# Moving two scans, one count and a few products inside a 24-step recurrent kernel

## The chip, the cores and the metric

The kernel runs on one core of a Trainium2 chip. The metric is the device time of one execution in microseconds (us). A core has five engines that run side by side, each through its own queue in order: TensorE (PE; its weight loads are shown as PEld), VectorE (DVE), ScalarE (ACT), GpSimd (POOL) and SyncE (SP). A unit waits for another only through semaphores. Matmul results land in a small memory of their own, PSUM, and are read from there by DVE and ACT; all other tiles lie in SBUF.

## The reference, cut to what matters

Three stages are computed on the host's inputs: a recurrent attention over 768 steps for 4 x 8 heads of width 40, a mixture of 8 experts over its 3072 output rows, and a feed-forward layer with a squared ReLU.

```
for t in range(S):                                  # S = 768, state is [B, H, D, D]
    y[:, :, t] = einsum('bhd,bhde->bhe', r_t, state)
    Sa = einsum('bhde,bhe->bhd', state, a_t)
    state = state * w_t[:, :, None, :] - einsum('bhd,bhe->bhde', Sa, b_t)
    state = state + einsum('bhd,bhe->bhde', v_t, k_t)

logits = x @ w_gate                                 # x = y, laid out as [3072, 320]
expert = argmax(logits); gate = softmax(logits)[expert]
pos[i] = number of earlier rows of the same expert  # rows beyond the capacity are dropped
out[i] = gate[i] * relu(x[i] @ w1[expert]) @ w2[expert]

h = maximum(out @ w_in, 0.0); result = (h * h) @ w_out
```

The change concerns the first stage, and of the second only the counting behind `pos`.

## The kernel before, in words

The 768 steps are cut into 24 chunks of 32 steps (c = 0 to 23), and `Attention.run` writes every engine's instructions out by hand, chunk by chunk; no scheduler moves them. Chunks 1 to 19 are written by the inner function `chunk(c)`, and chunk 0 and chunks 20 to 23 by the code behind it. `m = c % 4` is the place in a group of four.

In one chunk TensorE goes through the same list of products, each into a PSUM tile named in the trace: `pu` (L399), `py` (L489, the output of the chunk before), `pk` (transposes, L341), `G` (L192, the Gram product for the chunk seven ahead), `ps` (L418, the new state), `pv` (L455), `pq` (L467, scores), `px` (L385, the block product with the inverse, in `solve`), `gpt` (L845), `pa` (L341), `pn` (L441) and `pl` (L861, gate logits). DVE and ACT carry the results on: `gram_mask` reads G into `GM` and `N` (L205, L206), `state_decay` reads ps into `ru` (L429), `gate_in` reads py into `xt` (L498), `scores_mask` reads pq (L475); ACT copies pv to `vut` (L458), px to `lu` (L388), pl to `lg` (L862).

Four things set the order around the change.

- **The inverse.** Each group of four chunks needs one inverse of triangular blocks. When the last G of the group is masked, in the chunk with m = 0, `inv_start` transposes GM (L214) and prepares 27 products; `inv` then does a number of them (a product L265 and its sum L269, both on DVE, each needing the one before) at the end of the chunks with m = 0, 1 and 2. `PLAN` gives the numbers: 13, 9, 3 and, after `choose`, 2. With the last one `inv_end` writes `TT` (L304), which ACT copies into `TB` (L313, `block_T`) for px. `FIRST` is the plan of the first group and is not changed.
- **Scans and scalings.** `scan(c + 8)` does two running products over a tile `e` and its partner `wB` on DVE (L157, L160, L162, L163), and `scale` multiplies three parts of `e` on POOL (L178), once per chunk. The four quarters of the next `e` are loaded by four DMAs that ACT's queue issues (`load`, L138).
- **The gate's batches.** Rows are ranked in batches. At m = 3 of chunks 3, 7, 11 and 15 a batch is counted: `choose` (L882 to L890, DVE) at the end of the chunk before, `count` in the chunk (an exponential on ACT L895, eight matmul passes into `pc` L899, a copy on ACT L901), and `rank` and `rank_batch` (small DVE instructions, L908 to L938) at its end.
- **Small PSUM tiles.** py, pc, pq, gpt and pl come from `small`, which hands out two buffers in turn. So each of these tiles has to wait until the tile two before it in the program has been read.

Of the kernel before, what the change touches and what calls it, by code (L numbers as in the profile page):

```python
# [35 lines left out]
class Attention:  # L36
# [91 lines left out]
    def load(self, c, part=None):  # L128
        if c >= NC:
            return  # L130
        if not part:
            self.st["E", c] = self.eb(c % 8, [104, 2048], F32)
        e = self.st["E", c]
        if part is None:
            self.nc.sync.dma_start(e, self.E[c][:, 0:2048])
        else:
            s = slice(512 * part, 512 * part + 512)
            self.nc.scalar.dma_start(e[:, s], self.E[c][:, s])  # L138
# [373 lines left out]

    def run(self, extra, weights):
        LA, SHIFT = 7, 20
        PLAN, FIRST = (13, 9, 3, 2), (9, 10, 6, 2)
        V, G = self.nc.vector, self.nc.gpsimd
        gate = self.gate

        def fill(c, i):
            if 1 <= c <= 2:  # L520
                extra(5 * c + i, 5 * c + i + 1)
            elif 5 <= c < 14 and i == 2:
                extra(10 + c, 11 + c if c < 13 else None)

        def wload(i):
            r = (self.L, self.Tt)[i % 2].rearrange("p a b -> p (a b)")
            weights.load(i, r[:, 0:704], 1)
# [57 lines left out]
        def chunk(c):  # L585

            m, bt = c % 4, gate.batch(c)
            plan = FIRST if c < 4 else PLAN
            early, nxt = bt if c < 17 else None, gate.batch(c + 1) if c < 16 else None
            self.u(c)  # L590
            if bt and 17 <= c:
                gate.choose(*bt)
            self.y(c - 1)
            self.nat_k(c + 1)
            if m != 3:
                self.block_T(c + 1)
            self.load_r(c + 1)
            self.load(c + LA + 2, 0)
            fill(c, 0)
            self.gram(c + LA)  # L600
            self.gram_mask(c + LA)
            self.state(c)
            self.vu_t(c)
            if m == 3:
                self.block_T(c + 1)
            self.load(c + LA + 2, 1)
            fill(c, 1)
            if early:
                gate.count(*early)
            self.scan(c + LA + 1)  # L610
            self.scale(c + LA + 1)
            self.state_decay(c)
            self.gate_in(c - 1)
            self.scores(c)
            self.scores_mask(c)
            if m == 0:
                self.inv_start(c // 4 + 1, lambda k, h: G)
            self.solve(c + 1)
            self.load_v(c + 2)
            self.store_x(c - 1)  # L620
            self.load_w(c + LA + 4)
            self.load(c + LA + 2, 2)
            fill(c, 2)
            gate.xT(c - 1)
            if bt and 17 <= c:
                gate.count(*bt)
            self.nat_n(c + 2)
            self.nat_a(c + 2)
            self.nat_pc(c + 2)
            self.state_t(c + 1)  # L630
            self.load(c + LA + 2, 3)
            fill(c, 3)
            gate.logits(c - 1)
            if m != 3:
                self.inv("v" * plan[m])
            if nxt:
                gate.choose(*nxt)
            if m == 2:
                self.inv("v" * plan[3])
            if bt:  # L640
                gate.rank(*bt)
                gate.rank_batch(*bt)
            fill(c, 4)
            gate.scatter(1)
            if c == 19:
                wload(0)
                wload(1)
# [5 lines left out]
        for c in range(NC - 1):  # L653
            if 1 <= c < SHIFT:
                chunk(c)
                continue
            m = c % 4
# [90 lines left out]
        c = NC - 1  # L748
# [922 lines left out]
```

## Time and profile before

| | |
|---|---|
| Time, median of 3 runs | 1120.45 us (1119.92 to 1125.08) |
| Profiled execution, its own time | 1126.1 us |
| Its span, first to last instruction | 1124.2 us |
| Busy share of the span: PE, PEld, DVE, ACT, POOL | 83%, 75%, 69%, 50%, 24% |
| From 493.80 us to the end (experts and last layer) | 630.40 us, PE busy 595.29 us |
| Mean granted TensorE clock | 0.904 of full |

In the timelines below a row is one instruction or a run of like ones: start in us from the span's beginning, duration in us, engine, source line, operation, output <- inputs, shape, count, and in brackets the idle time of that engine before it with what ended it. "issue" as what ended it means that the profile shows no instruction whose end released the engine. The idle time in a row of a busy engine matters; that of an engine that nothing waits for does not.

### The profile page before, as it was taken

What the parts mean: (1) busy time and instruction counts of PE and PEld (TensorE: products, weight loads), DVE (VectorE), ACT (ScalarE), POOL (GpSimd) and SP (SyncE); (2) the same over time, 40 slices, a digit from 0 to 9 for tenths busy, and PEclk for the clock granted to TensorE, in tenths of its full rate; (3) what the DMA queues carried; (4) which work ended last, traced back from release to release, by engine and by line L of the source; (5) the groups of instructions that cost most, each with busy time, mean ns of one, the idle gap of its engine ahead of it and who ended that gap; (6) DMA issues with size and microseconds to landing.
All of it is one profiled execution on the core that took longest, in us unless ns stands there. A gap on an engine that the chain in (4) does not pass through costs nothing.

```text
span 1124.2 us, 30643 instructions
## 1 busy us (share of the span) xinstructions
PE 934.6 (83%) x12526; PEld 842.7 (75%) x12526; DVE 774.2 (69%) x1611; ACT 560.4 (50%) x1286; POOL 273.8 (24%) x320
## 2 busy tenths in 40 slices
PE   5247677778666788889889999799999999999995
PEld 3237566667665677768879999798899999999895
DVE  7999979889798795465887888876644344444432
ACT  7135464555463767634545566546634343434432
POOL 5422131222313101013554555423401010000000
PEclk6578888797797988899989999999999999999998
DMA  7736544444442223236765666534100001000000
GB/s 184 194 97 184 172 125 124 124 140 149 115 149 84 87 61 104 79 93 181 222 209 187 208 212 216 178 98 143 50 24 24 24 12 37 1 24 2 19 5 27
DMA packets 80647, 122.71 MB, mean 109 GB/s; under 512 B 9679, under 2 KB 57409, under 8 KB 79561
## 3 DMA queue, kind: packets, MB, share of 16 engines
q1 hardware_dynamic: 71173, 100.09, 30.2%
q10 hardware_dynamic: 7020, 12.78, 3.8%
q0 software_dynamic: 2304, 7.78, 2.2%
q8 instruction: 101, 1.65, 0.6%
q14 instruction: 49, 0.40, 0.1%
HBM read 91.36 MB, written 29.35 MB: 107 GB/s over the span
## 4 chain that ended last, share of the span: by engine, by line
PE 54%; DVE 18%; DMA 6%; issue 6%; ACT 5%; POOL 1%; SPq 1%; ACTq 0%; DVEq 0%; POOLq 0%
PE phg L1334 15%; PE phe L1334 5%; PE pog L1359 5%; PE pog L1360 5%; PE pog L1358 5%; DVE pr L265 4%; PE px L385 3%; DMA xs<-zs_s 2%; PE pq L467 2%; PE poe L1360 2%; PE poe L1358 2%; PE poe L1359 2%; DVE Tt L269 1%; DVE ru L429 1%; DVE Xm L269 1%
## 5 line engine op out<-in xcount | busy, mean ns | idle before, releaser
L1344 DVE SCALAR_TENSOR_TENSOR sqg<-phg,rg 128x512 f32<-128x512 f32 x96 | 66.2, 690 | 119.0 <-ACT rg L1343 119.0
L1343 ACT ACTIVATE rg<-phg 128x512 f32<-128x512 f32 x96 | 57.2, 596 | 110.5 <-PE phg L1334 110.3
L1346 DVE TENSOR_TENSOR hlg<-sqg,hhg 128x512 fp32r<-128x512 f32 x96 | 66.5, 693 | 65.9 <-ACT hhg L1345 63.2
L1345 ACT CAST hhg<-sqg 128x512 fp32r<-128x512 f32 x96 | 59.6, 621 | 78.5 <-DVE sqg L1344 78.5
L1334 PE MATMUL phg<-xhg,e 128*128 128x512 f32 x264 | 93.1, 393 | 0.0
L385 PE MATMUL px<-TB,X 128*104 128x128 f32 x384 | 67.2, 347 | 26.2 <-ACT TB L313 25.0
L388 ACT COPY lu<-px 104x512 f32<-104x512 f32 x48 | 25.7, 588 | 120.5 <-PE px L385 120.5
L385 PEld LDWEIGHTS px<-TB,X 128*104 128x104 f32 x384 | 61.7, 230 | 28.8 <-ACT TB L313 25.4
L467 PE MATMUL pq<-rq,vut 128*64 128x64 f32 x768 | 42.1, 264 | 49.0 <-issue 31.7
L178 POOL TENSOR_TENSOR e<-e 104x512 f32<-104x512 f32 x21 | 27.9, 1331 | 207.4 <-DVE e L163 90.2
L467 PEld LDWEIGHTS pq<-rq,vut 128*64 128x64 f32 x768 | 35.7, 173 | 55.0 <-issue 32.2
L1359 PE MATMUL pog<-e,hhg 128*128 128x320 f32 x240 | 74.1, 309 | 0.0
L1360 PE MATMUL pog<-e,hlg 128*128 128x320 f32 x240 | 74.1, 309 | 0.0
L1358 PE MATMUL pog<-e,hhg 128*128 128x320 f32 x240 | 73.9, 308 | 0.0
L192 PE MATMUL G<-e 64*32 64x64 f32 (+1 forms) x1536 | 27.6, 254 | 49.3 <-issue 29.2
L192 PEld LDWEIGHTS G<-e 64*32 64x32 f32 (+1 forms) x1536 | 20.1, 120 | 59.3 <-issue 33.6
L1152 POOL TENSOR_TENSOR e<-rw,e 128x256 fp32r<-128x256 f32 x51 | 43.0, 846 | 72.3 <-ACT e L1151 71.5
L1334 PE MATMUL phe<-xhe,e 128*128 128x480 f32 (+4 forms) x176 | 59.3, 378 | 0.0
L178 POOL TENSOR_TENSOR e<-e,wB 104x512 f32<-104x512 f32 x42 | 53.4, 1287 | 24.3 <-DVE wB L157 17.1
L1334 PEld LDWEIGHTS phg<-xhg,e 128*128 128x128 f32 x264 | 49.5, 188 | 8.8
L313 ACT COPY TB<-TT 32x256 f32<-32x256 f32 x94 | 37.8, 402 | 35.6 <-DVE TT L304 34.3
L1338 ACT ACTIVATE hhe<-phe 128x480 fp32r<-128x480 f32 (+4 forms) x64 | 33.9, 529 | 38.7 <-PE phe L1334 38.2
(315 smaller groups left out, 2919.5 us busy)
## 6 DMA issues: line engine op xcount, KB each, us to landing
e<-in_E_dram ACTq DMA_DIRECT2D x60, 208.0 KB
rw<-in_w_dram SPq DMA_DIRECT2D x30, 320.0 KB
zs_s<-zt SPq DMA_DIRECT2D x24, 320.0 KB
rw<-in_w_dram SPq DMA_DIRECT2D x30, 256.0 KB
e<-in_E_dram SPq DMA_DIRECT2D x9, 832.0 KB
ru<-in_VR_dram SPq DMA_DIRECT2D x48, 128.0 KB
cr<-in_wi_dram SPq DMA_DIRECT2D x20, 256.0 KB
cr<-in_wo_dram SPq DMA_DIRECT2D x20, 256.0 KB
```

Of the source, the lines that this page charges most:

```text
L178: eng.tensor_tensor(z, z, f, ALU.mult)
L192: T.matmul(gps[32 * g : 32 * g + 32, par, 64 * o : 64 * o + 64], e[r, 32 * i : 32 * i + 32], e[r, 512 + 64 * i : 576 + 64 * i], start=True ...
L385: self.nc.tensor.matmul(px[0:104, par, 128 * o : 128 * o + 128], X[:, par, o, :], TB[:, 4 * par + o, :], start=True, stop=True)
L467: T.matmul(pq[s, 64 * q : 64 * q + 64], vut[:, q, s], rt[:, :, q, pp], start=True, stop=True)
L1334: T.matmul(o, lt, rt, start=(i == 0), stop=(i == len(seq) - 1))
L1343: A.activation(r[:, :n], o, AF.Relu)
L1344: V.scalar_tensor_tensor(sq[:, :n], o, 0.0, r[:, :n], ALU.max, ALU.mult)
L1345: A.copy(hh[:, :n], sq[:, :n])
L1346: V.tensor_tensor(hl[:, :n], sq[:, :n], b32(hh)[:, :n], ALU.subtract)
L1358: T.matmul(o, hh[:, t], W["h2"], start=(f == 0), stop=False)
L1359: T.matmul(o, hh[:, t], W["l2"], start=False, stop=False)
L1360: T.matmul(o, hl[:, t], W["h2"], start=False, stop=(f == NF - 1))
```

## The change

Four edits, all in `Attention`.

- `gate.count` for the batches of chunks 3, 7, 11 and 15 is written behind `solve(c + 1)` in place of before the scan.
- For m = 0 and c >= 4 the scan and the scaling of chunk c + 8 are no longer in the chunk's middle: the chunk before, m = 3, does them at its very end, behind `rank_batch` (`scan(c + LA + 2)` there is the same tile). This concerns the tiles of chunks 12, 16 and 20; later ones don't exist.
- In chunks with m = 3 the fourth quarter of the next `e`, which the scan reads, is loaded first.
- `PLAN` becomes 15, 8, 2 and 2.

```
-        if not part:
+        if ("E", c) not in self.st:
             self.st["E", c] = self.eb(c % 8, [104, 2048], F32)
...
-        PLAN, FIRST = (13, 9, 3, 2), (9, 10, 6, 2)
+        PLAN, FIRST = (15, 8, 2, 2), (9, 10, 6, 2)
...
+            order = (3, 0, 1, 2) if m == 3 else (0, 1, 2, 3)
...
-            self.load(c + LA + 2, 1)
+            self.load(c + LA + 2, order[1])
             fill(c, 1)
-            if early:
-                gate.count(*early)
-            self.scan(c + LA + 1)
-            self.scale(c + LA + 1)
+            if m or c < 4:
+                self.scan(c + LA + 1)
+                self.scale(c + LA + 1)
             self.state_decay(c)
             self.gate_in(c - 1)
             self.scores(c)
...
             self.solve(c + 1)
+            if early:
+                gate.count(*early)
...
             if bt:
                 gate.rank(*bt)
                 gate.rank_batch(*bt)
+            if m == 3:
+                self.scan(c + LA + 2)
+                self.scale(c + LA + 2)
             fill(c, 4)
             gate.scatter(1)
```

TensorE's order in chunk 7 (m = 3) before; the digit in a name is the chunk it belongs to (px8 is the block product for chunk 8, pc2 the count of the batch that starts with chunk 2), and the brackets name the engines whose semaphores the instruction waits for:

```order
L455 MATMUL pv7_3063<-ident0_59,vu1_115 80x64 [waits PE_49,Activation_49]
...
L899 MATMUL pc2_3088<-oh_412,mats_384 128x32 [waits DVE_49]
L899 MATMUL pc2_3088<-oh_412,mats_384 128x32 x3
L467 MATMUL pq7_3107<-rq1_119,vut_117 64x64 [waits DMAHW0_49,DMAHW6_49,DVE_49,Activation_49]
L467 MATMUL pq7_3107<-rq1_119,vut_117 64x64 [waits Activation_49]
...
L385 MATMUL px8_3126<-TB0_110,X0_106 104x128 [waits PE_49,Activation_49]
...
L845 MATMUL gpt6_3146<-ident0_59,xt6_3105 128x128 [waits Activation_49]
```

The same place after:

```order
L455 MATMUL pv7_3063<-ident0_59,vu1_115 80x64 [waits PE_49,Activation_49]
...
L467 MATMUL pq7_3099<-rq1_119,vut_117 64x64 [waits DMAHW6_49,DMAHW0_49,Activation_49]
L467 MATMUL pq7_3099<-rq1_119,vut_117 64x64 [waits Activation_49]
...
L385 MATMUL px8_3118<-TB0_110,X0_106 104x128 [waits DVE_49,PE_49,Activation_49]
...
L904 MATMUL pc2_3130<-oh_412,mats_384 128x32 [waits DVE_49]
L904 MATMUL pc2_3130<-oh_412,mats_384 128x32 x3
L850 MATMUL gpt6_3146<-ident0_59,xt6_3097 128x128 [waits DVE_49,PE_49]
```

The count stands behind px; the first matmul of pq no longer waits for DVE, and the first of gpt now does.

DVE from the end of chunk 7 to the start of the inverse in chunk 8 before; the first row is the last of `rank_batch`:

```order
L938 RECIPROCAL gate_413<-sm_2_3218 128x4
L205 TENSOR_TENSOR GM_108<-G15_3325,mM_88 128x256
L206 TENSOR_TENSOR N15_3358<-G15_3325,mN_87 128x256
L157 SCALAR_TENSOR_TENSOR wB16_2506<-wB16_2506,onesB_82 104x512
L160 TENSOR_TENSOR Pc16_3415<-wB16_2506,e0_2992 104x16
L162 RECIPROCAL zR_83<-Pc16_3415 104x16
L163 SCALAR_TENSOR_TENSOR e0_2992<-e0_2992,zR_83 104x512
L429 TENSOR_TENSOR ru1_113<-ps8_3361,Pc9_1164 40x16x40 x2
L498 TENSOR_TENSOR xt7_3424<-py7_3272,Pn7_2530 128x320
L475 TENSOR_TENSOR rq0_118<-pq8_3426,mQ_89 64x512 x2
L214 STREAM_TRANSPOSE L_122<-GM_108 128x32x32
```

The same stretch after:

```order
L943 RECIPROCAL gate_413<-sm_2_3218 128x4
L157 SCALAR_TENSOR_TENSOR wB16_2512<-wB16_2512,onesB_82 104x512
L160 TENSOR_TENSOR Pc16_3233<-wB16_2512,e0_2992 104x16
L162 RECIPROCAL zR_83<-Pc16_3233 104x16
L163 SCALAR_TENSOR_TENSOR e0_2992<-e0_2992,zR_83 104x512
L205 TENSOR_TENSOR GM_108<-G15_3333,mM_88 128x256
L206 TENSOR_TENSOR N15_3366<-G15_3333,mN_87 128x256
L429 TENSOR_TENSOR ru1_113<-ps8_3369,Pc9_1164 40x16x40 x2
L498 TENSOR_TENSOR xt7_3424<-py7_3280,Pn7_2536 128x320
L475 TENSOR_TENSOR rq0_118<-pq8_3426,mQ_89 64x512 x2
L214 STREAM_TRANSPOSE L_122<-GM_108 128x32x32
```

The scan of chunk 16 stands ahead of the masking of G15, no longer between it and the state's decay.

DVE from the last products of chunk 8 to the first of chunk 9 before (the second number in pr3_12 is the product's):

```order
L265 TENSOR_TENSOR pr3_12_3558<-Xm_124,Tt_123 128x256
L269 TENSOR_REDUCE Tt_123<-pr3_12_3558 128x8x4
L205 TENSOR_TENSOR GM_108<-G16_3654,mM_88 128x256
...
L498 TENSOR_TENSOR xt8_3753<-py8_3601,Pn8_2843 128x320
L475 TENSOR_TENSOR rq1_119<-pq9_3755,mQ_89 64x512 x2
L265 TENSOR_TENSOR pr3_13_3850<-Xm_124,Tt_123 128x128
```

and after:

```order
L269 TENSOR_REDUCE Tt_123<-pr3_12_3558 128x8x4
L265 TENSOR_TENSOR pr3_13_3561<-Xm_124,Tt_123 128x128
L269 TENSOR_REDUCE Tt_123<-pr3_13_3561 128x8x4
L265 TENSOR_TENSOR pr3_14_3564<-Xm_124,Tt_123 128x128
L269 TENSOR_REDUCE Tt_123<-pr3_14_3564 128x8x4
L205 TENSOR_TENSOR GM_108<-G16_3660,mM_88 128x256
...
L498 TENSOR_TENSOR xt8_3759<-py8_3607,Pn8_2846 128x320
```

Products 13 and 14 stand ahead of chunk 9's masking, decay and xt in place of behind them; product 22 moves in the same way from chunk 10 to chunk 9.

## Rows read from the trace of the kernel before

**Rows 1.** Windows by engine: from:to length, PE, PEld, DVE, ACT, POOL busy, PEclk, DMA, GB/s.

```profile
234.71:288.26 53.55, 38.03 (x1108) 33.88 (x1106) 50.89 (x95) 30.43 (x74) 13.16 (x12) 0.79 0.47 141
...
251.70:270.40 18.70, 16.81 (x379) 15.07 (x380) 17.88 (x32) 9.08 (x22) 5.50 (x6) 0.54 0.42 126
```

**Rows 2.** Timeline of DVE, chunk 7 (m = 3) and chunk 8 (m = 0).

```profile
210.24 1.21 DVE L157 TENSOR_TENSOR_SCAN wB<-wB,onesB 104x512 f32<-104x512 f32 x1
...
213.14 1.63 DVE L429 TENSOR_TENSOR ru<-ps,Pc 40x640 f32<-40x640 f32 x2
214.78 0.49 DVE L498 TENSOR_TENSOR xt<-py,Pn 128x320 f32<-128x320 f32 x1
217.47 1.39 DVE L475 TENSOR_TENSOR rq<-pq,mQ 64x512 f32<-64x512 f32 x2 [2.20 <-PE pq L467]
...
227.28 0.42 DVE L205 TENSOR_TENSOR GM<-G,mM 128x256 f32<-128x256 f32 x1 [4.13 <-PE G L192]
...
233.29 1.39 DVE L475 TENSOR_TENSOR rq<-pq,mQ 64x512 f32<-64x512 f32 x2 [0.28 <-PE pq L467]
```

**Rows 3.** Timeline of PE, the same two chunks.

```profile
208.72 1.08 PE L899 MATMUL pc<-oh,mats 128*128 128x32 f32 x8
215.38 2.05 PE L467 MATMUL pq<-rq,vut 128*64 128x64 f32 x32 [5.57 <-issue]
217.35 2.56 PE L385 MATMUL px<-TB,X 128*104 128x128 f32 x16
219.75 0.49 PE L845 MATMUL gpt<-ident,xt 128*128 128x128 f32 x3
...
226.56 0.68 PE L192 MATMUL G<-e 64*32 64x64 f32 x43 [1.97 <-issue]
...
231.79 1.46 PE L467 MATMUL pq<-rq,vut 128*64 128x64 f32 x29 [1.11 <-issue]
```

**Rows 4.** Timeline of ACT, chunk 7.

```profile
208.92 1.06 ACT L458 COPY vut<-pv 80x512 f32<-80x512 f32 x2 [4.73 <-PE pv L455]
...
210.01 1.64 ACT L313 COPY TB<-TT 32x256 f32<-32x256 f32 x4
```

**Rows 5.** Timeline of DVE, xt in chunks 3, 11 and 15.

```profile
142.31 0.49 DVE L498 TENSOR_TENSOR xt<-py,Pn 128x320 f32<-128x320 f32 x1
...
287.77 0.49 DVE L498 TENSOR_TENSOR xt<-py,Pn 128x320 f32<-128x320 f32 x1
...
361.39 0.49 DVE L498 TENSOR_TENSOR xt<-py,Pn 128x320 f32<-128x320 f32 x1
```

**Rows 6.** Timeline of PE, gpt in chunks 3, 11 and 15, and pq in 11.

```profile
147.63 0.49 PE L845 MATMUL gpt<-ident,xt 128*128 128x128 f32 x3
...
288.36 1.97 PE L467 MATMUL pq<-rq,vut 128*64 128x64 f32 x32 [6.81 <-issue]
...
293.73 0.49 PE L845 MATMUL gpt<-ident,xt 128*128 128x128 f32 x3
...
366.40 0.49 PE L845 MATMUL gpt<-ident,xt 128*128 128x128 f32 x3
```

**Rows 7.** Timeline of DVE, chunks 9 and 10 (m = 1 and 2): products and `choose`.

```profile
253.05 0.80 DVE L265 TENSOR_TENSOR pr<-Xm,Tt 128x128 f32<-128x128 f32 x1
...
254.94 0.69 DVE L265 TENSOR_TENSOR pr<-L,Tt 128x512 f32<-128x512 f32 x1
...
270.97 1.51 DVE L265 TENSOR_TENSOR pr<-Xm,Tt 128x512 f32<-128x512 f32 x1
...
273.24 0.77 DVE L265 TENSOR_TENSOR pr<-Xm,Tt 128x320 f32<-128x320 f32 x1
...
275.90 0.17 DVE L882 TENSOR_REDUCE mx<-lg 128x4 f32<-128x32 f32 x1
```

**Rows 8.** Timelines of PE in chunk 9 and of ACT in chunk 10.

```profile
251.77 0.55 PE L845 MATMUL gpt<-ident,xt 128*128 128x128 f32 x3 [2.05 <-DVE xt L498]
...
274.79 0.15 ACT L862 COPY lg<-pl 128x8 f32<-128x8 f32 x1
```

More of the change, by code (lines that the diff above doesn't have):

```diff
@@ L597, in chunk @@
             self.load_r(c + 1)
-            self.load(c + LA + 2, 0)
+            self.load(c + LA + 2, order[0])
             fill(c, 0)
@@ L621, in chunk @@
             self.load_w(c + LA + 4)
-            self.load(c + LA + 2, 2)
+            self.load(c + LA + 2, order[2])
             fill(c, 2)
@@ L630, in chunk @@
             self.state_t(c + 1)
-            self.load(c + LA + 2, 3)
+            self.load(c + LA + 2, order[3])
             fill(c, 3)
```

## The prediction

> **What bounds the kernel now.** I read the page's list of lines first: everything behind the attention is one dense stretch of TensorE work that no edit touches, so its length stands and only its start can move. Then windows by group of four chunks. From the start of an inverse (L214 in chunk 8) to xt in chunk 11 DVE is busy 50.89 of 53.55 us [rows 1]; the rest is the gap of some 0.03 us between instructions, so DVE alone sets these 53.6 us, and the groups of chunks 4 and 12 have the same length. What is left of a group, from xt in the chunk with m = 3 to the next L214, is some 19 to 20 us with DVE idle in two places: 2.20 us before L475, waiting for pq, and 4.13 us before L205, waiting for G [rows 2]. There the path runs through TensorE and ACT: pq, px, gpt, then G, ps, pv, pq of the next chunk. So the timelines of those two stretches decide.
>
> In them the reader is to see one thing. In chunk 7 `vut`, which pq reads, is ready at 208.92 + 1.06 = 209.98 [rows 4], and TensorE has nothing else to do after pc. Yet pq starts at 215.38 behind 5.57 us of idling that the trace calls issue [rows 3]. xt ends at 214.78 + 0.49 = 215.27, 0.11 us earlier [rows 2]. In chunk 11 xt ends at 288.26 and pq starts at 288.36 [rows 5, 6], 0.10 us later. That is a wait for a PSUM buffer: with pc between py and pq, pq gets py's buffer, which DVE frees only with xt, 5 us behind because DVE comes late out of the inverse. In chunks without a count pq takes pl's old buffer and starts when vut is there. The order after shows the DVE wait gone from pq.
>
> **The change part by part.**
>
> *Count behind the block product.* pq starts when vut is there, and px when TB is: in chunk 7 TB ends at 210.01 + 1.64 = 211.65 [rows 4]. pq and px then run while DVE does scan, ru and xt. Now gpt is late next: it needs xt, and it takes pq's buffer, which L475 frees. L475 no longer waits 2.20 us and follows xt directly: it starts about 0.45 us after xt's start and takes 1.39 us, so gpt starts about 1.9 us after xt's start. Against the rows before:
> chunk 3: 142.31 + 1.9 = 144.2 in place of 147.63, 3.4 us;
> chunk 7: 214.78 + 1.9 = 216.7 in place of 219.75, 3.1 us;
> chunk 11: 287.77 + 1.9 = 289.7 in place of 293.73, 4.0 us;
> chunk 15: 361.39 + 1.9 = 363.3 in place of 366.40, 3.1 us [rows 2, 3, 5, 6].
> Sum 13.6 us. Behind gpt the chain to the next L214 is the same work, so it moves as a whole. The matmuls of pc (1.08 us, [rows 3]) now stand between px and gpt; they need xt too, and lie beside L475. The exponential and the copy on ACT go behind the two lu copies and stand ahead of gxT, which waits for gpt anyway.
>
> *Scan of chunks 12, 16, 20.* One scan takes 213.14 - 210.24 = 2.90 us of DVE [rows 2]. It leaves a place in m = 0 where it costs almost nothing: L475 in chunk 8 waited only 0.28 us for pq, so with the scan gone pq still sets L214. It goes into the 4.13 us that DVE idles before L205. Does it fit? `rank` and `rank_batch` end 4.13 us before 227.28, at 223.15, having begun with L475's end at 218.86: 4.3 us. After, L475 ends with gpt's start; rank 4.3 (up to 1 us later, if ACT's copy of pc is late) and scan 2.9 make 7.2 to 8.2 us. G ends at 227.24, which is 7.5 us behind gpt's start [rows 2, 3]. So L205 is at most 0.7 us late, and from G's end to pq's end (231.79 + 1.46) there are 6.0 us, for which DVE without the scan needs 233.01 - 2.90 - 227.28 = 2.8: 3.2 us to spare. I take 0. Bounds: a gain of 0.3 at three places, or, were the quarter of `e` not there in time, a loss of what exceeds those 3.2 us. That quarter is now issued first, a whole chunk ahead of its reader; POOL's three scalings wait for the last one, and behind them only a scatter that nothing in these chunks reads. SP's queue keeps its order.
>
> *15, 8, 2, 2.* The 27 products and their sum of time stay, so L214 to TT keeps its length. But in m = 1 masking, ru and xt come later by two products, 254.94 - 253.05 = 1.9 us, and in m = 2 by one, 273.24 - 270.97 = 2.3 us [rows 7]. TensorE in chunk 9 already waited 2.05 us for xt before gpt [rows 8], so it lags the full 1.9 us from there, through chunk 10 into chunk 11. DVE itself waits in two places at most. `choose` in chunk 10 starts at 275.90 and needs lg, ready at 274.79 + 0.15 = 274.94 [rows 7, 8]: 1.0 us of slack against 1.9, a loss of 0.9. In chunk 7, TB stands behind vut on ACT: with 1.9 us of lag TB ends at 209.98 + 1.9 + 1.64 = 213.5, px (2.56) at 216.1, pc (1.08) at 217.2, half a microsecond behind 216.7. I take 0.9 for chunk 11 and 0.6 for chunk 7, none for chunk 15, and nothing for chunk 3, whose plan is not changed.
>
> Sum: 13.6 - 1.5 = 12.1 us. The profiled execution takes 1126.1 us, with a span of 1124.2; 1126.1 - 12 = 1114. It lies 5.65 us above the median of 1120.45, and I carry the difference over: 1120.45 - 12 = **1108.5 us**.
>
> One rule speaks against the change. The trace first: behind the 2.05 us wait in chunk 9 the granted clock of the next 18.7 us is 0.54, nearly all at the lower level of 1.2 GHz [rows 1, 8]. The wait there grows to 3.9 us, and waits of 1.6 to 2 us appear in chunks 5 and 13. The Trainium skill, "TensorE: Matmul & The Clock Gate" (HAM oscillation: how this bites in real kernels), says that waits which recur between short bursts of matmuls put the array back to half its clock each time. By that rule TensorE would be late in every middle chunk, not only in chunk 9; that is the slower rival below.
>
> **The rivals.**
>
> *A, as above:* 1108.5, own range 1105 to 1112. For it: 0.10 and 0.11 us between xt and pq; against it: several chains of nearly equal length in the chunk with m = 3.
>
> *B, half is given back.* TB and px, or rank with the scan behind it, become the last to arrive in the chunk with m = 3, so each place gains 1.5 instead of 3 us: 4 x 1.5 = 6, and 1114.5. For it: px is only half a microsecond from being last in chunk 7. Against: chunks 3 and 15 have no such lag or no scan.
>
> *C, more than that.* The idle time before pq goes, TensorE keeps the higher clock, and pq and px shrink from 2.05 and 2.56 us [rows 3], which also speeds the way to G: 1 us more at each place, 16 us, 1104.5.
>
> *D, it does not act.* The wait called issue is the engine's instruction supply, and remains: 1120.5. For it: that name, and 1.97 us of the same name before G. Against: the 0.1 us behind xt.
>
> *E, slower.* TensorE lags so far behind DVE in m = 1 and 2 that `choose` waits for lg in chunks 6, 10 and 14. The price is each microsecond beyond the slack, 1.0 in chunk 10; it decides when three such waits exceed the 12 us won, over 4 us each. If the lower clock held in all three and TensorE's 16.81 us of the 18.70 us window [rows 1] grew by half, lg would be some 7 us late, 3 x 7 - 12 = 9 us slower: 1129. Against: chunk 9 to 10 already ran at 0.54 and lg was still early.
>
> **How the numbers follow.** A 0.55, B 0.20, C 0.10, D 0.08, E 0.07. A measurement of this kernel can tell about 0.5%, 5.6 us, from no change. Faster by that is under 1114.85: A, C and most of B, 0.80. Same: D and the rest of B, 0.13. Slower: E, 0.07. The range for 8 in 10 goes from 1104 (the lower half of C out) to 1116 (nearly all of B in).
>
> **What would show it.** In the profile after: pq in chunks 3, 7, 11, 15 some 0.1 us behind vut or the buffer of pl, not behind xt; gpt there right behind L475; no idle time before L475 in these chunks; the idle time before L205 in chunks 4, 8, 12 down from over 4 us to about 1; the time from L214 to xt in the fourth chunk 53.6 us, or up to 1 us more with a wait before L882; L214 of chunks 4, 8, 12, 16 earlier by about 3.4, 6, 9 and 12 us. I am wrong if pq still starts behind xt, if DVE waits on TensorE inside the inverse, or if the start of the experts moves by less than the chunks did.

## The result, and the profile after

The changed kernel takes 1110.01 us (median of 16 runs, 1103.31 to 1119.22) against 1122.44 us for the kernel before, run beside it on the same chip (16 runs, 1113.79 to 1128.63). The ratio is 0.9884, with a 95% interval of 0.9859 to 0.9909: 13 us faster, between 10.2 and 15.8 us. The forecast was 12 us. The profiled execution of after takes 1111.79 us with a span of 1109.9 us, that of before 1126.1 us.

DVE after, chunks 7 and 8, answering to [rows 2]:

```profile
212.72 0.49 DVE L498 TENSOR_TENSOR xt<-py,Pn 128x320 f32<-128x320 f32 x1
213.13 1.38 DVE L475 TENSOR_TENSOR rq<-pq,mQ 64x512 f32<-64x512 f32 x2
...
219.12 1.19 DVE L157 TENSOR_TENSOR_SCAN wB<-wB,onesB 104x512 f32<-104x512 f32 x1
...
222.12 0.42 DVE L205 TENSOR_TENSOR GM<-G,mM 128x256 f32<-128x256 f32 x1
...
223.31 1.66 DVE L429 TENSOR_TENSOR ru<-ps,Pc 40x640 f32<-40x640 f32 x2 [0.43 <-PE ps L418]
...
226.62 1.39 DVE L475 TENSOR_TENSOR rq<-pq,mQ 64x512 f32<-64x512 f32 x2 [1.13 <-PE pq L467]
228.04 2.18 DVE L214 STREAM_TRANSPOSE L<-GM 128x1024 f32<-128x1024 f32 x1
```

The wait of 2.20 us before L475 and that of 4.13 us before L205 are both gone; waits of 0.43 and 1.13 us for ps and pq have come. PE in the same two chunks, answering to [rows 3]:

```profile
207.86 0.33 PE L467 MATMUL pq<-rq,vut 128*64 128x64 f32 x2 [0.75 <-ACT vut L458]
208.34 1.15 PE L467 MATMUL pq<-rq,vut 128*64 128x64 f32 x30 [0.15 <-ACT vut L458]
210.01 1.99 PE L385 MATMUL px<-TB,X 128*104 128x128 f32 x16 [0.52 <-ACT TB L313]
...
213.27 1.08 PE L904 MATMUL pc<-oh,mats 128*128 128x32 f32 x8 [1.27 <-DVE xt L498]
214.66 0.52 PE L850 MATMUL gpt<-ident,xt 128*128 128x128 f32 x3 [0.31 <-DVE rq L475]
...
221.24 0.66 PE L192 MATMUL G<-e 40*32 40x64 f32 x41 [1.73 <-issue]
```

pq now starts right behind vut, and px behind TB, both ahead of xt; gpt waits for L475 and starts 1.94 us behind xt's start. What DVE waited for between 140 and 430 us (chunk 3 to chunk 20); the columns are us in total, times and the longest. Before:

```profile
DVE GM L205 <- PE G L192: 17.8, 4, 5.1
DVE rq L475 <- PE pq L467: 11.0, 6, 2.2
```

and after:

```profile
DVE rq L475 <- PE pq L467: 10.6, 5, 3.5
DVE mx L887 <- ACT lg L867: 3.7, 4, 2.6
DVE ru L429 <- PE ps L418: 3.5, 5, 1.4
DVE GM L205 <- PE G L192: 2.9, 3, 2.1
```

The four groups from L214 of chunk 0 to L214 of chunk 16 as one window, before:

```profile
89.72:380.44 290.72, 205.12 (x6043) 184.52 (x6044) 247.38 (x513) 158.16 (x386) 72.40 (x61) 0.83 0.45 133
```

and after:

```profile
91.87:368.68 276.81, 209.90 (x6036) 186.93 (x6037) 248.97 (x514) 159.99 (x386) 72.38 (x61) 0.84 0.48 140
```

DVE does the same 247 to 249 us of work in 276.81 us in place of 290.72, so the 13.91 us between the two are idle time of DVE that went (43.34 us before, 27.84 after), less 1.59 us more of work. L214 of chunks 4, 8, 12 and 16, counted from L214 of chunk 0, is 4.40, 8.82, 10.69 and 13.91 us earlier; forecast were 3.4, 6, 9 and 12. The next table divides these windows by four marks that stand in each group; every number is a sum over the four groups, from the starts of the rows in the timelines (in us). The last column goes on from L214 of chunk 0 to xt of chunk 19. Each row comes from one profiled execution.

| kernel | xt (m = 3) to gpt | gpt to L205 | L205 to L214 | L214 to xt (m = 3) | to xt of 19 |
|---|---|---|---|---|---|
| before | 21.26 | 28.92 | 28.63 | 211.91 | 336.09 |
| after | 7.75 | 28.88 | 27.19 | 212.99 | 322.19 |
| count alone (e1) | 8.09 | 31.23 | 28.99 | 211.88 | 325.50 |
| scans alone (e2) | 20.75 | 27.88 | 25.47 | 211.68 | 331.12 |
| plan alone (e3) | 22.44 | 28.98 | 29.14 | 212.48 | 338.36 |
| buffer alone (e4) | 6.62 | 28.84 | 28.93 | 211.87 | 321.62 |
| after, old plan (e5) | 7.74 | 31.71 | 27.50 | 211.89 | 324.15 |
| after, wait put back (e7) | 26.29 | 30.48 | 26.07 | 212.15 | 340.34 |
| buffer and scans (e8) | 6.10 | 31.41 | 26.96 | 211.99 | 321.87 |

### The profile page after: what moved, and what is told of

Same layout as the page of the kernel before. It is cut to its first block, busy times and chain, and to the rows that moved or that the text cites. A ratio compares the mean times of both kernels' runs of the same rounds, so it can differ in the third digit from the quotient of the medians.

```text
span 1109.9 us, 30636 instructions
## 1 busy us (share of the span) xinstructions
PE 939.7 (85%) x12526; PEld 844.4 (76%) x12526; DVE 773.8 (70%) x1611; ACT 562.1 (51%) x1286; POOL 274.2 (25%) x320
## 4 chain that ended last, share of the span: by engine, by line
PE 50%; DVE 27%; DMA 8%; issue 7%; ACT 4%; SPq 2%; POOL 2%; ACTq 0%; DVEq 0%; POOLq 0%
PE phg L1339 16%; PE pog L1364 5%; PE pog L1365 5%; PE pog L1363 5%; DVE pr L265 4%; PE phe L1339 3%; DMA e<-in_E_dram 2%; DVE ru L429 2%; PE px L385 2%; DMA xs<-zs_s 2%; DVE Tt L269 2%; DVE Xm L269 2%; DVE rq L475 2%; DVE pr L297 1%; DVE e L163 1%
## 5 line engine op out<-in xcount | busy, mean ns | idle before, releaser
L467 PEld LDWEIGHTS pq<-rq,vut 128*64 128x64 f32 x768 | 33.2, 158 | 29.9 <-ACT vut L458 27.4
L1365 PE MATMUL poe<-e,hle 128*120 128x320 f32 (+4 forms) x150 | 47.3, 316 | 6.1 <-DVE hle L1344 6.1
```

The source lines that it names most:

```text
L467: T.matmul(pq[s, 64 * q : 64 * q + 64], vut[:, q, s], rt[:, :, q, pp], start=True, stop=True)
L1365: T.matmul(o, hl[:, t], W["h2"], start=False, stop=(f == NF - 1))
```

## The experiments

All were timed in five rounds beside the kernel before. The number behind "Measured" is the ratio to the time of that kernel, with its 95% interval.

**e1_count: the count alone.**

```
-            if early:
-                gate.count(*early)
             self.scan(c + LA + 1)
...
             self.solve(c + 1)
+            if early:
+                gate.count(*early)
```

> The kernel before with one edit: the count is written behind the block product; scans and plan stay. Theory 1 (the gain is the wait of pq for the PSUM buffer that xt frees, at four places): all of the gain, 11 to 14 us off the kernel before, ratio about 0.989; pq starts about 0.1 us behind vut, gpt about 1.9 us behind xt. Theory 2 (the gain is the work of DVE taken out of the chunk with m = 0 and spread anew): 0 to 2 us off, ratio 0.998 to 1.000. Theory 3 (the idle time called issue is the supply of instructions): no change, the 5 us before pq stay or appear before px.

Measured: 0.9899 (0.9867 to 0.9932), 11 us. The count alone brings nearly the whole gain, and xt to gpt shrinks by 13.2 us, nearly as in after (13.5). PE in chunk 7, where xt starts at 209.35 us:

```profile
203.40 1.15 PE L467 MATMUL pq<-rq,vut 128*64 128x64 f32 x30 [0.15 <-ACT vut L458]
205.83 3.37 PE L385 MATMUL px<-TB,X 128*104 128x128 f32 x16 [1.29 <-ACT TB L313]
```

pq and px no longer wait for xt. The theory of the DVE balance and that of the instruction supply fall.

**e2_scan: the scans alone.** The edits of the change without count and plan.

```
-            self.scan(c + LA + 1)
-            self.scale(c + LA + 1)
+            if m or c < 4:
+                self.scan(c + LA + 1)
+                self.scale(c + LA + 1)
...
+            if m == 3:
+                self.scan(c + LA + 2)
+                self.scale(c + LA + 2)
```

> The kernel before with the scans and scalings of chunks 12, 16 and 20 at the end of the chunk before, and the load order that goes with them; count and plan stay. Theory 1: 0 to 1 us off, since L475 in chunks 4, 8 and 12 waits for pq in any case and pq still waits for xt in the fourth chunk. Theory 2: three scans of 2.90 us leave DVE's path, 8 to 9 us off, ratio 0.992.

Measured: 0.9957 (0.9932 to 0.9982), 4.8 us. Neither number holds. DVE in chunk 8 of this kernel:

```profile
223.53 0.42 DVE L205 TENSOR_TENSOR GM<-G,mM 128x256 f32<-128x256 f32 x1 [1.03 <-PE G L192]
...
224.89 1.66 DVE L429 TENSOR_TENSOR ru<-ps,Pc 40x640 f32<-40x640 f32 x2 [0.61 <-PE ps L418]
...
228.06 1.39 DVE L475 TENSOR_TENSOR rq<-pq,mQ 64x512 f32<-64x512 f32 x2 [0.99 <-PE pq L467]
229.48 2.14 DVE L214 STREAM_TRANSPOSE L<-GM 128x1024 f32<-128x1024 f32 x1
```

From L205 to L214 it is 5.95 us. With the scan between L205 and ru it is 7.06 us in e4, without any wait in it:

```profile
219.37 0.42 DVE L205 TENSOR_TENSOR GM<-G,mM 128x256 f32<-128x256 f32 x1 [2.63 <-PE G L192]
...
220.04 1.22 DVE L157 TENSOR_TENSOR_SCAN wB<-wB,onesB 104x512 f32<-104x512 f32 x1
...
222.94 1.63 DVE L429 TENSOR_TENSOR ru<-ps,Pc 40x640 f32<-40x640 f32 x2
...
225.01 1.38 DVE L475 TENSOR_TENSOR rq<-pq,mQ 64x512 f32<-64x512 f32 x2
```

So DVE, not pq, sets L214 there as long as the scan stands in it, and its removal is worth 1.1 us until ps and pq are late in its place. Of the 4.94 us by which L214 of chunk 16 comes earlier in this profile, 2.79 lie from L205 to L214 in the three chunks that lose a scan; what the rest is was not taken apart.

**e3_plan: the plan alone.**

```
-        PLAN, FIRST = (13, 9, 3, 2), (9, 10, 6, 2)
+        PLAN, FIRST = (15, 8, 2, 2), (9, 10, 6, 2)
```

> The kernel before with the plan 15, 8, 2 and 2 alone. Theory 1: 0 to 2 us slower (the wait of choose for the gate logits in chunk 10, and none won), ratio 1.000 to 1.002. Theory 2: some us faster, since DVE idles less before L205.

Measured: 0.9985 (0.9962 to 1.0008), no difference that can be measured. In its profile, counted from L214 of chunk 0, xt of chunk 19 is 2.3 us later than before, and the first product of the experts 1.5 us earlier.

**e4_rotate: only the buffer.** `ns` is the counter by which `small` hands out its two PSUM buffers.

```
             if early:
                 gate.count(*early)
+                self.ns += 1
```

> The kernel before with one counter raised by one behind the count, so that in chunks 3, 7, 11 and 15 pq takes the small PSUM buffer that pc had in place of that of py. No instruction is moved on any engine. Theory 1: pq starts about 0.1 us behind vut, gpt waits for xt alone and starts right behind it, 0.3 us behind xt's end, so 12 to 16 us off, ratio 0.986 to 0.989. Theory 2 and theory 3 (order or supply of instructions): no change, ratio 1.000.

Measured: 0.9879 (0.9838 to 0.9920), 13.6 us: as much as the whole change, without an instruction moved. ACT, PE and DVE in chunk 7:

```profile
206.80 0.25 ACT L902 COPY pr<-pc 128x128 f32<-128x128 f32 x1
...
207.10 1.84 PE L467 MATMUL pq<-rq,vut 128*64 128x64 f32 x32 [2.58 <-ACT pr L902]
208.87 2.88 PE L385 MATMUL px<-TB,X 128*104 128x128 f32 x16
211.59 0.49 PE L846 MATMUL gpt<-ident,xt 128*128 128x128 f32 x3
...
210.23 0.49 DVE L498 TENSOR_TENSOR xt<-py,Pn 128x320 f32<-128x320 f32 x1
```

xt starts at 210.23, so pq no longer waits for it. It waits for pr instead, the copy by which ACT empties pc's buffer, and the trace names that wait, where it called the one for xt "issue". gpt starts 1.36 us behind xt's start, behind px, and not 0.3 us behind xt's end as expected.

**e5_oldplan: after with the plan of before.** `PLAN` is 13, 9, 3, 2 again.

> The changed kernel with the plan 13, 9, 3 and 2 put back: count and scans moved, plan as before. Theory 1 (the plan itself is worth nothing or costs the 1 to 2 us by which TensorE lags in the fourth chunk and choose waits for the gate logits): ratio against the kernel before 0.985 to 0.989, no wait of over 0.5 us before L887 in chunk 10. Rival (the plan is part of the gain): ratio 0.990 or above.

Measured: 0.9873 (0.9828 to 0.9917), the same as after within the intervals. The plan is no part of the gain. From L214 to xt it is 53.12, 53.08 and 53.08 us in the groups of chunks 4, 8 and 12; after has 53.30, 53.64 and 53.54, 1.20 us more.

**e7_waitback: after with the wait put back.**

```
+            if early:
+                self.ns += 1
             self.scores(c)
```

> The changed kernel with one counter raised by one ahead of the scores in chunks 3, 7, 11 and 15, so that pq takes the PSUM buffer of py again, which xt frees; every instruction stays in its place. Theory 1: the wait comes back, pq about 0.1 us behind xt, and with it most of the 13.5 us from xt to gpt; scans and plan keep some 2 to 4 us, so ratio 0.995 to 0.998. Rival (the place of the count in the order is what matters): unchanged, ratio 0.988.

Measured: 0.9990 (0.9962 to 1.0017). The gain is gone, although every instruction stands where it does in after. DVE and PE in chunk 7:

```profile
214.90 0.49 DVE L498 TENSOR_TENSOR xt<-py,Pn 128x320 f32<-128x320 f32 x1
...
215.49 1.98 PE L467 MATMUL pq<-rq,vut 128*64 128x64 f32 x32 [6.70 <-issue]
217.40 3.74 PE L385 MATMUL px<-TB,X 128*104 128x128 f32 x16
220.93 1.12 PE L906 MATMUL pc<-oh,mats 128*128 128x32 f32 x8
221.89 0.53 PE L852 MATMUL gpt<-ident,xt 128*128 128x128 f32 x3
```

xt starts at 214.90 and lasts 0.49 us, so pq follows its end by 0.10 us, as before. The expectation that scans and plan keep 2 to 4 us was not met: pc now also stands between the late px and gpt (about 1 us in each of four places), and xt to gpt is 5 us longer than before, which takes back the 2.6 us that L205 to L214 is shorter. So e7 shows that the wait is back; its ratio holds this price of pc beside the wait.

**e8_rot_scan: e4 and e2 together**, with the plan of before.

> The kernel before with the counter raised behind the count (pq takes pc's PSUM buffer, nothing moved) and the scans of chunks 12, 16 and 20 at the end of the chunk before; plan as before. Theory 1 with the scan's price as the scan alone showed it (1.1 us from L205 to L214 at three places, and 0.8 to 1 us from xt to gpt at four places less than in the changed kernel): 14 to 18 us off the kernel before, ratio 0.984 to 0.988. Rival (the two gains are the same time, since both end in the wait of DVE for G): ratio as with the rotation alone, 0.988 to 0.990.

Measured: 0.9841 (0.9799 to 0.9882), which is what theory 1 expected. But the interval overlaps that of e4, and in its profile xt of chunk 19 stands at 321.87 us against 321.62 in e4. Whether the scans add anything to the buffer is not settled: gpt to L205 is 2.57 us longer than in e4, which takes back the 1.97 us won from L205 to L214, and no run shows why.

**e9_inv_early: fill what is left.** In after and e8 DVE waits for ps and pq before L475 with the inverse's first step, which needs neither, queued behind. Against e8:

```
             self.gram_mask(c + LA)
+            if m == 0:
+                self.inv_start(c // 4 + 1, lambda k, h: G)
...
             self.scores_mask(c)
-            if m == 0:
-                self.inv_start(c // 4 + 1, lambda k, h: G)
```

> The kernel of e8_rot_scan with the transpose L214 that begins the inverse written right behind the masking of G (L205, L206) in place of behind L475. The 0.4 us that DVE then waits for ps and the 1.1 us for pq are covered by the transpose of 2.1 us, so 1.5 us less at each of five places: 5 to 8 us below e8_rot_scan, ratio to the kernel before 0.978 to 0.982. Rival (ru, xt and L475 come 1.5 us later and TensorE, which needs ru for pn, loses what DVE wins, or choose waits for the logits): ratio as e8_rot_scan or above.

Measured: 0.9774 (0.9735 to 0.9813), 25 us less than before, a little below the expected 0.978. By the medians it is 7.1 us below e8, though the two intervals overlap. DVE in chunk 8:

```profile
221.41 0.42 DVE L205 TENSOR_TENSOR GM<-G,mM 128x256 f32<-128x256 f32 x1
...
222.08 2.12 DVE L214 STREAM_TRANSPOSE L<-GM 128x1024 f32<-128x1024 f32 x1
224.08 1.61 DVE L429 TENSOR_TENSOR ru<-ps,Pc 40x640 f32<-40x640 f32 x2
...
226.86 1.39 DVE L475 TENSOR_TENSOR rq<-pq,mQ 64x512 f32<-64x512 f32 x2 [0.64 <-PE pq L467]
```

The transpose lies where DVE waited for ps, and of the wait for pq 0.64 us is left. The edit acts in chunks 4, 8, 12 and 16, four places and not the five of the expectation. In these the waits for ps, 3.27 us in e8, are gone, but those for pq only go from 6.25 to 4.44 us, 1.87 and 1.93 of it in chunks 4 and 12. xt of chunk 19 is at 317.77 us, 4.1 us below e8. Another 6.8 us of the difference between the two profiles lie from there to the experts, in code that the edit does not touch, so what of the 7.1 us is the edit's is not known.

**e10_inv_fill: the first five products too.**

```
             self.scores(c)
+            if m == 0:
+                self.inv("v" * 5)
             self.scores_mask(c)
...
-                self.inv("v" * plan[m])
+                self.inv("v" * (plan[m] - 5 * (m == 0)))
```

> The kernel of e9_inv_early with the first five of the inverse's 27 products, 2.4 us of small DVE instructions that need neither pq nor xt, written ahead of L475 in chunks 4, 8, 12 and 16 in place of behind it. Theory 1 (what DVE idles there is the chain from G to pq, and any independent work fills it): the waits of L475 of 1.87, 0.64 and 1.93 us in chunks 4, 8 and 12 go, 4 to 5 us less than e9_inv_early, ratio to the kernel before 0.973 to 0.976. Rival (rq comes 1.5 us later and TensorE, by now as late as DVE, gives it back at the next G): as e9_inv_early, 0.977.

Measured: 0.9766 (0.9716 to 0.9815), the best kernel of all by its median, 1094.64 us, and just above the expected 0.976; by the intervals it can't be told from e9. Its waits of DVE between 140 and 430 us:

```profile
DVE GM L205 <- PE G L192: 6.3, 4, 2.1
DVE rq L475 <- PE pq L467: 5.6, 3, 3.5
```

The waits for pq in chunks 4, 8 and 12 are gone, xt of chunk 19 is at 314.07 us, 3.7 us below e9, and one wait for G of 2.13 us has come in chunk 13: both theories hold in part.

## Why the prediction was right

*The wait for the PSUM buffer.* Shown from both sides: taking it away alone gives the whole gain (e4), putting it back alone takes the gain away (e7, where some 4 us of the loss are pc behind the late px). The rival that "issue" was the supply of instructions is out for pq in chunks 3, 7, 11 and 15; other waits of that name remain.

*The count, 13.6 us.* Measured from xt to gpt: 21.26 - 7.75 = 13.51 us, 3.38, 3.03, 4.03 and 3.07 in the four places, against 3.4, 3.1, 4.0 and 3.1. gpt follows xt by 1.93 or 1.94 us in each, as worked out. The chance that px or pc would be last (rival B) did not come: in chunk 7 px is done by 212.00, and pc waits 1.27 us for xt.

*The scans, 0 us.* This term was wrong. The step that failed is the one that took the 0.28 us which L475 waited in chunk 8 [rows 2] as proof that pq sets L214. That pq had 1.11 us of issue in it [rows 3], a gap that the other kernels have there with 0.42 us at most and chunks 4 and 12 of before not at all. There L475 follows xt without a wait, as the trace of before could have told:

```profile
160.26 1.38 DVE L475 TENSOR_TENSOR rq<-pq,mQ 64x512 f32<-64x512 f32 x2
...
306.83 1.38 DVE L475 TENSOR_TENSOR rq<-pq,mQ 64x512 f32<-64x512 f32 x2
```

Without the gap DVE's own chain of 7.06 us is the longer (e4), and the scan counts for 1.1 us, outside the bound of 0.3. In the profile of after the first two places have it (6.08 and 5.92 us from L205 to L214, 7.03 and 7.43 before); the third, 8.43 us against 7.05, gave it back. There TensorE was held up 1.70 us by issue, and its granted clock was 0.55 of full from 294.80 to 302.00 us, where chunk 7 has 1.00 from 207.80 to 214.60:

```profile
294.81 0.25 PE L455 MATMUL pv<-ident,vu 64*80 64x64 f32 x2 [1.70 <-issue]
295.79 2.45 PE L467 MATMUL pq<-rq,vut 128*64 128x64 f32 x32 [0.73 <-ACT vut L458]
298.17 3.74 PE L385 MATMUL px<-TB,X 128*104 128x128 f32 x16
```

px takes 3.74 us here and 1.99 us in chunk 7. So the term of 0 comes out near what was measured because a gain of 2.46 us in two places meets a loss of 1.38 in the third, and that is luck; 1.08 us of the three scans is left. The remaining 0.36 of the table's 1.44 us belongs to chunk 16, where no scan stood.

*The plan, -1.5 us.* Near in size, not right in its working. The wait before gpt in chunk 9, from which TensorE's lag was worked out, did not grow from 2.05 to 3.9 us but fell to 1.17. The wait before `choose` comes in all three groups and is small:

```profile
200.84 0.19 DVE L887 TENSOR_REDUCE mx<-lg 128x4 f32<-128x32 f32 x1 [0.21 <-ACT lg L867]
...
269.74 0.19 DVE L887 TENSOR_REDUCE mx<-lg 128x4 f32<-128x32 f32 x1 [0.42 <-ACT lg L867]
...
341.31 0.19 DVE L887 TENSOR_REDUCE mx<-lg 128x4 f32<-128x32 f32 x1 [0.44 <-ACT lg L867]
```

They make 1.07 of the 1.20 us by which after exceeds e5 there. The 0.6 us for px did not come.

*The slower rival.* TensorE did not lag as far as it needed. From xt to xt in the chunks with m = 1 and m = 2 of the groups of chunks 4, 8 and 12 there are six stretches; two of them after:

```profile
246.11:264.38 18.27, 14.17 (x379) 12.51 (x379) 17.53 (x27) 10.80 (x26) 4.99 (x5) 0.77 0.52 150
...
335.95:353.24 17.29, 14.36 (x373) 12.87 (x374) 16.15 (x28) 9.19 (x22) 5.01 (x5) 0.71 0.28 85
```

PEclk, the third number from the right, is 0.81, 0.80, 0.77, 0.80, 0.91 and 0.71 in the six, mean 0.80. In before it was 1.00, 0.73, 0.54, 0.87, 0.90 and 0.83, mean 0.81. The waits of gpt for xt in these six grew from 6.5 us in four to 11.2 us in all six. The Trainium skill, "TensorE: Matmul & The Clock Gate" (HAM oscillation: how this bites in real kernels), has a loop in which the wait behind every short burst of matmuls, longer than the burst itself, puts the array back to half its clock. The trace agrees in so far as none of the six is at the full clock any more, and differs in that the mean did not fall with the growing waits; in e5 it is 0.84 with 12.0 us of them. The waits here, 1.17 to 2.92 us, are also far shorter than the 12.6 to 14.4 us of PE work in each stretch. In the 23.60 us ahead of `choose` in chunk 14 (317.71 to 341.31) the granted clock was 0.82, and `choose` waited 0.44 us for the logits, not 7.

*On the way to the end.* From L214 of chunk 0 to the first product of the experts (`pte`) it was 404.15 us (89.72 to 493.87) and is 391.73 (91.87 to 483.60): 12.4 us of the 13.91 arrive. So one of the prediction's own signs of being wrong came, the experts moving by less than the chunks. The 1.5 us are lost from xt of chunk 19 to the experts (68.06 us before, 69.54 after), in code that the change does not touch and that takes 63.4 to 70.2 us in the other profiles. From the first product of the experts to the end, unchanged too, it is 630.33 us before, 626.30 after and 624.96 to 629.33 in the others. One profile therefore does not settle a few us in the whole, and that 12 us were forecast and 12.43 came between the medians is in part luck: the chunks gave 13.91 and not 12.1, and the 1.5 us behind them were not in the sum.

## What to carry to other kernels

An idle time that the profile calls issue, ending 0.1 us behind an instruction of another engine, may be a wait for a buffer, as it was here: find who had that buffer last, and try one turn more of the rotation before moving code. Read the slack of a chain from several of its repetitions, for one late matmul in one of them, as in chunk 8 here, makes another engine look idle. Where an engine idles at the end of a chain, look behind it in its queue for work that needs nothing of that chain.

## What the hardware showed beside this

Gaps called issue remain at G in every kernel, 14 to 17 of them between 85 and 490 us, 19 to 34 us in all, and no change of order took them away. PE after, those of chunks 6, 7 and 9:

```profile
184.73 0.51 PE L192 MATMUL G<-e 40*32 40x64 f32 x34 [1.87 <-issue]
...
204.66 0.51 PE L192 MATMUL G<-e 40*32 40x64 f32 x34 [0.69 <-issue]
...
234.43 0.66 PE L192 MATMUL G<-e 40*32 40x64 f32 x41 [1.18 <-issue]
```

They fall in the midst of G; others, of up to 2.2 us, fall in pv, pq, pu and py. The matmul passes between two gaps, summed over the rows and leaving out the waits of pq for xt, are 126 or 127, 252 or 253, or 379 to 382 in some 60% of the pairs in before and after (15 of 24 and 15 of 25), and in 10 to 15 of some 31 in e5, e7, e8 and e9: often a grid of about 126.5 passes. In before the 1.11 us in pq of chunk 8 lie 126 passes behind the gap in G (43 + 64 + 16 + 2 + 1). That may be the supply of instructions in blocks, three to a chunk of some 380 passes; no run took it apart, and the cause stays open.
